# VectorE's small chain behind the products with v, sixteen lead maxima between the last q blocks, the feature DFT with one change of w, wo in query buffers

## The chip, the cores and the metric

The kernel runs on one core of one Trainium2 chip. The metric is device microseconds of one execution: 1841.45 us, the median of 3 runs (1840.29 to 1842.69). A further execution was profiled; it took 1840.34 us, and its span, from the first to the last instruction, is 1838.6 us. Times in the text are microseconds from the start of that span unless a unit is named.

Engines: PE is TensorE (its weight loads are shown apart, as PEld), DVE is VectorE, ACT is ScalarE, POOL is GpSimd, SP is SyncE, which issues every DMA of this kernel from one queue.

## The reference

Everything is float32. x is [2048, 640]. A gate per token mixes a Fourier layer and an attention with 32 heads of 20 columns, which all share one key and one value:

```python
a = jnp.einsum("bsd,ed->bse", x, dft_hid_re)
b = jnp.einsum("bsd,ed->bse", x, dft_hid_im)
y = jnp.einsum("ts,bse->bte", dft_seq_re, a) - jnp.einsum("ts,bse->bte", dft_seq_im, b)

q = (x @ wq) as 32 heads of 20; k = x @ wk; v = x @ wv       # wk, wv: [640, 20]
p = softmax(q k^T * 20 ** -0.5)
o = (p v, heads side by side) @ wo

g = sigmoid((x * gate_w).sum(-1, keepdims=True))
out = g * y + (1 - g) * o
```

wq, wk, wv and wo are drawn 64 times as large as the other weights, so the scores are large and the softmax needs its row maximum.

## The kernel before, in words

**Precision.** float32 values are split into a high and a low part in a faster 32-bit type, and a product is made of three matmuls: high by high, high by low, low by high. A split is a cast and a subtraction, and each operand of a matmul is split once.

**Stages.**

1. The q stage (lines 224 to 352). Four token blocks n of 512. For each: k, v and the gate column (`kv_mm`, `kv_out`), then five q blocks m of 128 columns (`q_mm`, 15 matmuls of 512 columns each), each written to DRAM as a high and a low part (`q_out`). `kv_turn` transposes v. After the last block come `kv_turn(kvT, 3)` and five small instructions for the gate.
2. The lead loop (lines 813 to 828). 240 steps, each with one matmul of the feature DFT on either half of the array (`halves.run`), and spread over them 88 half units of maxima (`a_half`): LEAD is 12, NL is 2 * (32 + 12).
3. 256 rounds (lines 848 to 882): 16 pairs of heads, two query halves, eight steps. The order of TensorE's work within a round is written out by hand as a list (`AB15`, `Y16`, `Y12`, `N12`): bXSn is a half unit of scores, aXSn one of maxima, each on row half X of the array and in PSUM bank Sn, yX one matmul of the DFT, E evicts a finished DFT result, and V is the products with v of an earlier round. The first 48 rounds hold 15 steps of the feature DFT each, the next 144 hold 16 of the sequence DFT, the last 64 hold 12; `N12` is used once no maxima are left.
4. The output projection (lines 889 to 904): 32 groups of 15 matmuls of 320 columns, each evicted by VectorE with the gate and the row of y, and stored.

**Maxima before scores.** A query half v (1024 queries of one pair of heads) has 32 units u, each a block of 128 queries by 512 keys, for two heads. `a_unit` multiplies and VectorE reduces the maximum from PSUM into `mx`. When all 64 halves of v are there, a small chain on VectorE follows: `a_reduce` (L380), then in `a_final` a transpose (L388), a cast (L389) and a subtraction (L390). The result goes to DRAM (`m_d`) and comes back with four DMAs as rows 60, 61, 124 and 125 of `qs[v]`. There it meets keys of -1, so that the score matmul (62 rows) subtracts the maximum, and ScalarE's exponential follows (L735). Maxima run ahead of scores by the lead. In the kernel before, `a_half` puts `a_reduce` one tick and `a_final` two ticks after the last unit; a tick passes with every second half unit of scores.

**The DFT.** The feature DFT runs through four phases, (half, e): which 1024 tokens, and which 320 of the output columns. A change of e needs the other columns of the matrix w, loaded and split by GpSimd (`load_w`, `split_w`, L188 and L189). The order was (1,0), (1,1), (0,1), (0,0). The first phase is the lead loop, the other three the first 48 rounds. Results of half 1 are stored to DRAM and read back for the second half of the sequence DFT.

**Order.** TensorE, ScalarE, VectorE and GpSimd run in the order of the program. SyncE's order is laid out by the framework's scheduler, which may issue a transfer ahead of others that stand before it in the program; waits between instructions are also the framework's, by the memory that they touch.

**wo.** In the last half of the last pair, `BEFORE` lists what follows which of the eight rounds: `load_wo` for three blocks and then two, each with its DMA and its split on VectorE, the loads of the attention output (`load_o`), its multiplication by the reciprocal sums on GpSimd (`mult_o`) and its split (`split_o`, L507 and L508). The raw blocks of wo lay in `spare` tiles, two of them in the slots of the sequence DFT's matrix blocks.

Of the kernel before, what the change touches and what calls it, by code (L numbers as in the profile page):

```python
# [33 lines left out]
def kernel(  # L34
# [165 lines left out]

    PHASES = ((1, 0), (1, 1), (0, 1), (0, 0))
    XSEQ = [SJ * half + j for half, e in PHASES for j in range(SJ)]
# [21 lines left out]
    with ExitStack() as c1:  # L224
# [59 lines left out]

        def kv_turn(kvT, n):
# [8 lines left out]
            nc.vector.tensor_copy(  # L294
                gz[:, ns].rearrange("p (j o) -> p j o", o=1), pv[:, :, 2 * DH : 2 * DH + 1]
            )


        load_x1(0, 0)
# [22 lines left out]
        for n in range(1, 4):  # L322
            for c in range(KC):
                load_x1(n + 1, c)
            pkv = rot(f"kv_{n}")
            for c in range(KC):
                kv_mm(pkv, n, c)
            kv_turn(kvT, n - 1)
            kvT = kv_out(pkv, n)
# [16 lines left out]
        kv_turn(kvT, 3)  # L346

        nc.vector.tensor_scalar_max(gz, gz, -87.0)
        nc.scalar.activation(omg, gz, AF.Exp, scale=-1.0)
        nc.vector.tensor_scalar_add(omg, omg, 1.0)  # L350
        nc.vector.reciprocal(gate, omg)
        nc.vector.tensor_scalar(omg, gate, -1.0, 1.0, op0=ALU.mult, op1=ALU.add)


    abp = ctx.enter_context(tc.tile_pool(name="abp", bufs=1))
    sml = ctx.enter_context(tc.tile_pool(name="sml", bufs=2))

    mx = {}
    QB = NT // 2
    UV = 4 * QB  # L360

    def a_unit(u, hh, tag="A"):

        v, r = divmod(u, UV)
        qb, c = divmod(r, 4)
        if r == 0 and v not in mx:
            mx[v] = sml.tile([P, 2, QB, 4], F32, name="mx")
        b = 64 * hh
        ps = bank(tag, f"a_{u}_{hh}")
        nc.tensor.matmul(  # L370
            ps,
            qs[v][b : b + 60, qb * P : (qb + 1) * P],
            ks[b : b + 60, c * ROW : (c + 1) * ROW],
            start=True,
            stop=True,
        )
        nc.vector.tensor_reduce(mx[v][:, hh, qb, c : c + 1], ps, axis=AX.X, op=ALU.max)  # L377

    def a_reduce(v):
        nc.vector.tensor_reduce(  # L380
            mxr[v % 2][:, : 2 * QB], mx.pop(v).rearrange("p h q c -> p (h q) c"), axis=AX.X, op=ALU.max
        )

    def a_final(v):

        mt = sml.tile([P, 32], F32, name="mt")
        ms = sml.tile([P, 2, 32], F32R, name="ms")
        nc.vector.transpose(mt, mxr[v % 2])  # L388
        nc.vector.tensor_copy(ms[:, 0], mt)  # L389
        nc.vector.tensor_tensor(ms[:, 1], mt, ms[:, 0].bitcast(F32), op=ALU.subtract)  # L390
        move(m_d[v], ms)

        m_v = m_d[v].rearrange("(g r) i t -> r i g t", g=4)
        for hh in range(2):
            for i in range(2):
                r = 64 * hh + 60 + i
                move(
                    qs[v][r : r + 1].rearrange("o (b g t) -> o b g t", g=4, t=32),
                    m_v[hh * QB : (hh + 1) * QB, i : i + 1].rearrange("b o g t -> o b g t"),
                )  # L400


    clock = {"n": 0}
    todo = []

    def later(n, f, *args):
        todo.append((clock["n"] + n, f, args))

    def tick():
        clock["n"] += 1  # L410
        due = [t for t in todo if t[0] <= clock["n"]]
        todo[:] = [t for t in todo if t[0] > clock["n"]]
        for _, f, args in due:
            f(*args)

    NA = NPAIR * 64
    state = [0, 0]

    def a_half(hh, tag="A"):
        u = state[hh]  # L420
        if u >= NA:
            return
        a_unit(u, hh, tag)
        state[hh] = u + 1
        if state[1 - hh] <= u:
            return
        v, r = divmod(u, UV)
        if r == 8 and v + 1 < 2 * NPAIR:
            load_qs(v + 1)
        if r == UV - 1:  # L430
            later(1, a_reduce, v)
            later(2, a_final, v)


# [25 lines left out]
    def spare(k, name):  # L460
        if k % 4 < 2:
            return yp[0].tile([P, D], F32, tag=f"spare{k % 4}", name=name, bufs=1)
        return c_slot(k % 4, [P, D], F32, name)

    def load_wo(cs):
        for c in cs:
            raw = spare(c, "woraw")
            move(raw, wo[c * P : (c + 1) * P])
            t = abp.tile([P, 2, D], F32R, tag=f"ab{c}0", name=f"wo{c}")
            split_w = (t[:, 0], t[:, 1])  # L470
            nc.vector.tensor_copy(split_w[0], raw)
            nc.vector.tensor_tensor(split_w[1], raw, split_w[0].bitcast(F32), op=ALU.subtract)
            wos[c] = split_w

# [43 lines left out]
    def o_group(tb, e):  # L518
# [5 lines left out]
        for c in range(KC):  # L524
            mm3(ps, h[:, c, tk], l[:, c, tk], wos[c][0][:, es], wos[c][1][:, es], KC, c)
        oy = yp[0].tile([P, HALF], F32, tag=("yt", "yu")[e], name="oy")
# [221 lines left out]
    def finish_half(p, qh):  # L748
# [86 lines left out]
    def plan_of(n):  # L835
# [5 lines left out]

    BEFORE = {
        4: (lambda: load_wo(range(3)), lambda: load_o(0), lambda: load_o(1)),
        5: (lambda: load_wo(range(3, KC)), lambda: mult_o(0), lambda: mult_o(1)),
        6: (lambda: split_o(0), lambda: load_o(2)),
        7: (lambda: [load_y(tb) for tb in range(4)],),
    }
    old = []

    for rnd in ROUNDS:  # L850
# [29 lines left out]
        if p == LAST and qh == 1:  # L880
            for f in BEFORE.get(kk, ()):
                f()
    for g in range(2):
# [68 lines left out]
```

## Time and profile before

| what | value |
|---|---|
| median of 3 runs | 1841.45 us |
| profiled execution | 1840.34 us |
| its span | 1838.6 us |
| TensorE busy in it | 1804.0 us |
| VectorE, ScalarE, GpSimd busy | 1391.0, 1235.0, 555.3 us |
| products with v of round 1 start at | 173.28 us |
| products with v of the last round | 1752.74 us |

A line of a timeline or of a group reads: start and duration in us, engine, line of the kernel, operation, what it writes <- what it reads, shapes as partitions x elements, count; in brackets the idle time of the engine just before it and what ended that. A line of windows reads: from and to, length, the busy time of PE, PEld, DVE, ACT and POOL with their instructions, the granted TensorE clock (1 is full), DMA share and GB/s. "SPq" is SyncE's queue; in its lines of waits stand the total, the number and the longest.

### The profile page before, as it was taken

What the parts mean: (1) busy time and instruction counts of PE and PEld (TensorE: products, weight loads), DVE (VectorE), ACT (ScalarE), POOL (GpSimd) and SP (SyncE); (2) the same over time, 40 slices, a digit from 0 to 9 for tenths busy, and PEclk for the clock granted to TensorE, in tenths of its full rate; (3) what the DMA queues carried; (4) which work ended last, traced back from release to release, by engine and by line L of the source; (5) the groups of instructions that cost most, each with busy time, mean ns of one, the idle gap of its engine ahead of it and who ended that gap; (6) DMA issues with size and microseconds to landing.
All of it is one profiled execution on the core that took longest, in us unless ns stands there. A gap on an engine that the chain in (4) does not pass through costs nothing.

```text
span 1838.6 us, 42883 instructions
## 1 busy us (share of the span) xinstructions
PE 1804.0 (98%) x17112; PEld 1298.8 (71%) x17112; DVE 1391.0 (76%) x2313; ACT 1235.0 (67%) x2422; POOL 555.3 (30%) x495
## 2 busy tenths in 40 slices
PE   8998999999999999999999999999999999999989
PEld 6787667767767776777667767776776666666679
DVE  4387888888887888788878888888888888888144
ACT  3335777777777777677767767777777777777810
POOL 3057555665312122122221222222221222111122
PEclk9998999999999999999999999999999999999999
DMA  7643321121221112111111452212221112111366
GB/s 248 195 159 124 118 83 49 41 75 57 78 69 46 58 58 63 54 55 46 61 57 48 141 195 73 74 61 60 60 65 52 52 44 63 52 50 32 108 202 209
DMA packets 107300, 158.08 MB, mean 86 GB/s; under 512 B 25172, under 2 KB 76116, under 8 KB 106500
## 3 DMA queue, kind: packets, MB, share of 16 engines
q1 hardware_dynamic: 107100, 155.34, 26.8%
q8 instruction: 134, 2.20, 0.5%
q14 instruction: 66, 0.54, 0.1%
HBM read 110.80 MB, written 48.76 MB: 87 GB/s over the span
## 4 chain that ended last, share of the span: by engine, by line
PE 84%; DVE 7%; issue 5%; DMA 2%; POOL 1%; SPq 1%; ACT 0%; POOLq 0%; ACTq 0%; DVEq 0%
PE av L739 24%; PE y L545 19%; PE b L727 17%; PE a L370 13%; PE ab L545 5%; DVE mx L377 5%; PE o L116 1%; PE o L114 1%; PE o L115 1%; SPq L106 1%; PE q L114 1%; PE q L116 1%; PE q L115 1%; DVE ms L390 0%; DVE ms L389 0%
## 5 line engine op out<-in xcount | busy, mean ns | idle before, releaser
L377 DVE TENSOR_REDUCE mx<-a 128x1 f32<-128x512 f32 x2048 | 1277.8, 683 | 295.0 <-PE a L370 258.5
L735 ACT ACTIVATE pt<-b 128x512 f32<-128x512 f32 x2048 | 1076.4, 603 | 383.0 <-PE a L370 296.2
L727 PE MATMUL b<-qs,ks 62*128 62x512 f32 x2048 | 775.0, 417 | 10.9 <-DVE mx L377 8.1
L370 PE MATMUL a<-ks,qs 60*128 60x512 f32 x2048 | 732.5, 414 | 6.3 <-DVE mx L377 3.9
L545 PE MATMUL y<-ab,ch 64*128 64x320 f32 x4096 | 722.2, 307 | 0.0
L545 PEld LDWEIGHTS y<-ab,ch 64*128 64x128 f32 x4096 | 549.6, 185 | 10.0
L727 PEld LDWEIGHTS b<-qs,ks 62*128 62x128 f32 x2048 | 350.9, 185 | 242.4 <-DVE mx L377 198.9
L545 PE MATMUL y<-ab,cl 64*128 64x320 f32 x2048 | 510.2, 306 | 0.0
L739 PE MATMUL av<-pt,vsb 128*32 128x512 f32 x4096 | 492.9, 599 | 0.0
L370 PEld LDWEIGHTS a<-ks,qs 60*128 60x128 f32 x2048 | 353.0, 185 | 16.1 <-DVE mx L377 4.6
L545 PEld LDWEIGHTS y<-ab,cl 64*128 64x128 f32 x2048 | 320.9, 185 | 6.4
L555 POOL TENSOR_TENSOR yt<-yt,yu 128x320 f32<-128x320 f32 x64 | 55.8, 872 | 720.8 <-ACT yu L550 710.2
L739 PEld LDWEIGHTS av<-pt,vsb 128*32 128x32 f32 x4096 | 106.9, 109 | 224.1 <-issue 215.6
L447 POOL TENSOR_TENSOR cl<-craw,ch 128x1024 fp32r<-128x1024 f32 x62 | 148.1, 2389 | 5.0
L446 POOL CAST ch<-craw 128x1024 fp32r<-128x1024 f32 x62 | 64.5, 1041 | 262.7 <-PE y L545 209.6
L567 POOL TENSOR_TENSOR abt<-abt,abu 128x320 f32<-128x320 f32 x64 | 55.7, 871 | 143.3 <-ACT abu L589 143.3
L545 PE MATMUL ab<-wbh,xh 64*128 64x320 f32 x256 | 61.6, 310 | 0.0
L545 PE MATMUL ab<-wbh,xl 64*128 64x320 f32 x256 | 61.1, 309 | 0.0
L572 POOL TENSOR_TENSOR ab<-abt,ab 128x320 fp32r<-128x320 f32 x64 | 56.2, 877 | 13.1 <-ACT ab L571 6.4
L114 PE MATMUL o<-wo,osp 128*128 128x320 f32 x160 | 50.5, 315 | 4.5 <-DVE osp L507 4.5
L545 PE MATMUL ab<-w0l,xh 64*128 64x320 f32 x192 | 53.6, 317 | 1.0 <-POOL w0l L189 1.0
L545 PE MATMUL ab<-w1l,xh 64*128 64x320 f32 x192 | 51.8, 308 | 0.0
(96 smaller groups left out, 1466.6 us busy)
## 6 DMA issues: line engine op xcount, KB each, us to landing
craw<-in_cre_dram SPq DMA_DIRECT2D x32, 512.0 KB
craw<-in_cim_dram SPq DMA_DIRECT2D x32, 512.0 KB
xraw<-in_xT_dram SPq DMA_DIRECT2D x32, 320.0 KB
qs<-qh_d SPq DMA_DIRECT2D x128, 80.0 KB
ab_d<-ab SPq DMA_DIRECT2D x16, 640.0 KB
y_d<-yt SPq DMA_DIRECT2D x64, 160.0 KB
ab<-ab_d SPq DMA_DIRECT2D x16, 640.0 KB
xr<-in_xT_dram SPq DMA_DIRECT2D x20, 256.0 KB
```

The lines of the kernel that those rows point to most:

```text
L114: nc.tensor.matmul(ps, wh, xh, start=(i == 0), stop=False)
L370: nc.tensor.matmul(ps, qs[v][b : b + 60, qb * P : (qb + 1) * P], ks[b : b + 60, c * ROW : (c + 1) * ROW], start=True, stop=True,)
L377: nc.vector.tensor_reduce(mx[v][:, hh, qb, c : c + 1], ps, axis=AX.X, op=ALU.max)
L446: eng.tensor_copy(h, raw)
L447: eng.tensor_tensor(l, raw, h.bitcast(F32), op=ALU.subtract)
L545: nc.tensor.matmul(ps, w, x, start=start, stop=stop)
L555: nc.gpsimd.tensor_tensor(yt, yt, yu, op=ALU.add)
L567: nc.gpsimd.tensor_tensor(t0, t0, t1, op=ALU.add)
L572: nc.gpsimd.tensor_tensor(lo, t0, hi.bitcast(F32), op=ALU.subtract)
L727: nc.tensor.matmul(ps, ks[b : b + 62, kc * P : (kc + 1) * P], qs[2 * p + qc // 2][b : b + 62, (qc % 2) * ROW : (qc % 2 + 1) * ROW], start= ...
L735: nc.scalar.activation(t, ps, AF.Exp, scale=SCALE)
L739: nc.tensor.matmul(ps[32 * g : 32 * g + 32, :], vsb[:, kc, :], t, start=first, stop=last)
```

## The change

- `mx` comes from an early pool (`qsp`, two tiles) instead of `sml`, and the functions of the maxima move up in the program. During the last token block, after each of the first four q blocks, four half units of maxima are issued (16 in all), in banks S1 to S4; q blocks and transposes of this block keep to F1, V, S0 and F0. `kv_turn(kvT, 3)` and the gate's instructions follow the second q block.
- LEAD is 10: 84 half units run ahead, 68 of them in the lead loop.
- The order of phases is (1,0), (0,0), (1,1), (0,1).
- `a_reduce`, `a_final` and `finish_sums` go into a list `chores`, which is worked off after each `av_step` (V) of a round; in the lead loop it is worked off at once.
- wo's raw blocks take turns in two tiles; loads and splits stand apart, from round 0 to round 5 of the last half. The split parts of blocks 0 to 2 lie in the first three query buffers and a free slot of the sequence DFT's blocks, those of 3 and 4 in two `ab` tiles.

```diff
-    PHASES = ((1, 0), (1, 1), (0, 1), (0, 0))
+    PHASES = ((1, 0), (0, 0), (1, 1), (0, 1))
...
-            mx[v] = sml.tile([P, 2, QB, 4], F32, name="mx")
+            mx[v] = qsp.tile([P, 2, QB, 4], F32, tag=f"mx{v % 2}", name="mx", bufs=1)
...
+    chores = []
+
+    def do_chores():
+        while chores:
+            f, *args = chores.pop(0)
+            f(*args)
...
         if r == UV - 1:
-            later(1, a_reduce, v)
-            later(2, a_final, v)
+            chores.append((a_reduce, v))
+            chores.append((a_final, v))
+            if not stage["loop"]:
+                do_chores()
...
+            if n == 3:
+                rot = Rot(["F1", "V", "S0", "F0", "F1", "V", "S0", "F0"])
             pkv = rot(f"kv_{n}")
...
                 q_out(ps, n, m)
+                if n == 3 and m < KC - 1:
+                    for z in range(4):
+                        a_half(z % 2, f"S{1 + z}")
+                    if m == 1:
+                        kv_turn(kvT, 3, rot)
+                        gate_out()
...
+        return cpool.tile([P, D], F32, tag=f"raw{k % 4 - 2}", name=name)
+
+    wo_raw = {}
+
+    def load_wo(c):
+        wo_raw[c] = spare(c % 2, "woraw")
+        move(wo_raw[c], wo[c * P : (c + 1) * P])
+
+    def split_wo(c):
+        raw = wo_raw.pop(c)
+        if c < 3:
+            if c == 0:
+                wos["at"] = [t[:, : 3 * HALF] for t in qbuf[:3]]
+                wos["at"].append(c_slot(2 * free_c[0], [P, 3 * HALF], F32R, "wo"))
+            at = [wos["at"][k // 3][:, k % 3 * HALF : (k % 3 + 1) * HALF] for k in range(4 * c, 4 * c + 4)]
+        else:
+            t = abp.tile([P, 4, HALF], F32R, tag=f"ab{c - 3}0", name=f"wo{c}")
+            at = [t[:, k] for k in range(4)]
+        for e in range(2):
+            h, l, r = at[2 * e], at[2 * e + 1], raw[:, e * HALF : (e + 1) * HALF]
+            nc.vector.tensor_copy(h, r)
+            nc.vector.tensor_tensor(l, r, h.bitcast(F32), op=ALU.subtract)
+            wos[c, e] = (h, l)
...
-            later(24, finish_sums, p, sm)
+            later(24, chores.append, (finish_sums, p, sm))
...
-    LEAD = 12
+    LEAD = 10
...
-    done = 0
+    done = first = 2 * state[0]
...
-        while done < NL * n // KL:
+        while done < first + (NL - first) * n // KL:
...
     BEFORE = {
-        4: (lambda: load_wo(range(3)), lambda: load_o(0), lambda: load_o(1)),
-        5: (lambda: load_wo(range(3, KC)), lambda: mult_o(0), lambda: mult_o(1)),
-        6: (lambda: split_o(0), lambda: load_o(2)),
-        7: (lambda: [load_y(tb) for tb in range(4)],),
+        0: ((load_wo, 0), (load_wo, 1)),
+        1: ((split_wo, 0), (split_wo, 1), (load_wo, 2)),
+        2: ((load_wo, 3), (split_wo, 2)),
+        3: ((load_wo, 4),),
+        4: ((split_wo, 3), (load_o, 0), (load_o, 1)),
+        5: ((split_wo, 4), (mult_o, 0), (mult_o, 1)),
+        6: ((split_o, 0), (load_o, 2)),
+        7: tuple((load_y, tb) for tb in range(4)),
     }
...
                     av_step(*st)
+                    do_chores()
```

More of the change, by code (lines that the diff above doesn't have):

```diff
@@ L199, in w_of, with later, tick, a_unit @@
         return h[:, c], l[:, c]
-    PHASES = ((1, 0), (1, 1), (0, 1), (0, 0))
+    clock = {"n": 0}
+    todo = []
+    def later(n, f, *args):
+        todo.append((clock["n"] + n, f, args))
+    def tick():
+        clock["n"] += 1
+        due = [t for t in todo if t[0] <= clock["n"]]
+        todo[:] = [t for t in todo if t[0] > clock["n"]]
+        for _, f, args in due:
+            f(*args)
+    mx = {}
+    QB = NT // 2
+    UV = 4 * QB
+    def a_unit(u, hh, tag="A"):
+        v, r = divmod(u, UV)
+        qb, c = divmod(r, 4)
+        if r == 0 and v not in mx:
+            mx[v] = qsp.tile([P, 2, QB, 4], F32, tag=f"mx{v % 2}", name="mx", bufs=1)
+        b = 64 * hh
+        ps = bank(tag, f"a_{u}_{hh}")
+        nc.tensor.matmul(
+            ps,
+            qs[v][b : b + 60, qb * P : (qb + 1) * P],
+            ks[b : b + 60, c * ROW : (c + 1) * ROW],
+            start=True,
+            stop=True,
+        )
+        nc.vector.tensor_reduce(mx[v][:, hh, qb, c : c + 1], ps, axis=AX.X, op=ALU.max)
@@ new lines, in a_reduce, with a_final @@
+    def a_reduce(v):
+        nc.vector.tensor_reduce(
+            mxr[v % 2][:, : 2 * QB], mx.pop(v).rearrange("p h q c -> p (h q) c"), axis=AX.X, op=ALU.max
+        )
+    def a_final(v):
+        mt = sml[0].tile([P, 32], F32, name="mt")
+        ms = sml[0].tile([P, 2, 32], F32R, name="ms")
+        nc.vector.transpose(mt, mxr[v % 2])
+        nc.vector.tensor_copy(ms[:, 0], mt)
+        nc.vector.tensor_tensor(ms[:, 1], mt, ms[:, 0].bitcast(F32), op=ALU.subtract)
+        move(m_d[v], ms)
+        m_v = m_d[v].rearrange("(g r) i t -> r i g t", g=4)
+        for hh in range(2):
+            for i in range(2):
+                r = 64 * hh + 60 + i
+                move(
+                    qs[v][r : r + 1].rearrange("o (b g t) -> o b g t", g=4, t=32),
+                    m_v[hh * QB : (hh + 1) * QB, i : i + 1].rearrange("b o g t -> o b g t"),
+                )
@@ L296, in kv_turn, with gate_out @@
             )
+        def gate_out():
+            nc.vector.tensor_scalar_max(gz, gz, -87.0)
+            nc.scalar.activation(omg, gz, AF.Exp, scale=-1.0)
+            nc.vector.tensor_scalar_add(omg, omg, 1.0)
+            nc.vector.reciprocal(gate, omg)
+            nc.vector.tensor_scalar(omg, gate, -1.0, 1.0, op0=ALU.mult, op1=ALU.add)
         load_x1(0, 0)
@@ L379, in a_reduce @@
[L379 to L400, printed above, removed]
@@ L435 @@
+    sml.append(ctx.enter_context(tc.tile_pool(name="sml", bufs=2)))
     free_c = [0, 1, 2]
@@ L880 @@
         if p == LAST and qh == 1:
-            for f in BEFORE.get(kk, ()):
-                f()
+            for f, n in BEFORE[kk]:
+                f(n)
     for g in range(2):
```

80 lines of the change are left out of this document (19 added, 61 removed).

## The prediction

> **What bounds the kernel now.** I read the page first, then windows by stage, then the timelines of the windows that stood out.
>
> ```profile
> span 1838.6 us, 42883 instructions
> PE 1804.0 (98%) x17112; PEld 1298.8 (71%) x17112; DVE 1391.0 (76%) x2313; ACT 1235.0 (67%) x2422; POOL 555.3 (30%) x495
> PE 84%; DVE 7%; issue 5%; DMA 2%; POOL 1%; SPq 1%; ACT 0%; POOLq 0%; ACTq 0%; DVEq 0%
> ```
>
> TensorE sets the end, yet its 98% busy says little: two half-array matmuls overlap, so a late start hides as long as anything runs. Losses show in start times. The profiled execution took 1840.34 us, its span 1838.6 plus 1.7 around it; the median of the runs shown is 1841.45, 1.1 above. The sum below starts from 1840.34.
>
> The pace of one matmul with 320 columns comes from the output projection, where each result closes 15 of them; the pace of one round comes from the last rounds, which hold no maxima:
>
> ```profile
> 1826.34 0.55 DVE L527 SCALAR_TENSOR_TENSOR oy<-o,omg,yrow 128x320 f32<-128x320 f32 x1 [1.65 <-PE o L116]
> 1828.54 0.55 DVE L527 SCALAR_TENSOR_TENSOR oy<-o,omg,yrow 128x320 f32<-128x320 f32 x1 [1.65 <-PE o L116]
> ...
> 1747.99 1.92 PE L739 MATMUL av<-pt,vsb 128*32 128x512 f32 x16
> 1749.85 0.73 PE L727 MATMUL b<-qs,ks 62*128 62x512 f32 x4
> 1752.74 1.92 PE L739 MATMUL av<-pt,vsb 128*32 128x512 f32 x16
> ```
>
> 2.20/15 = 0.147 us a matmul. Sixteen products with v hold TensorE 1.86 us (1747.99 to 1749.85), four score halves at most 0.73, and such a round takes 4.75.
>
> **Part 1: sixteen lead maxima go between the q blocks.** The lead stage:
>
> ```profile
> 97.43 0.69 DVE L263 TENSOR_TENSOR ql<-q,qh 128x512 fp32r<-128x512 f32 x1 [2.81 <-ACT qh L262]
> 101.80 3.08 DVE L377 TENSOR_REDUCE mx<-a 128x1 f32<-128x512 f32 x5 [2.44 <-DMA qs<-qh_d]
> 102.55 0.49 PE L370 MATMUL a<-ks,qs 60*128 60x512 f32 x1 [3.27 <-DVE mx L377]
> 106.62 0.19 PEld L370 LDWEIGHTS a<-ks,qs 60*128 60x128 f32 x1
> 110.42 0.18 PEld L370 LDWEIGHTS a<-ks,qs 60*128 60x128 f32 x1
> 106.00:155.00 49.00, 48.35 (x521) 46.37 (x518) 48.89 (x84) 22.23 (x51) 35.92 (x37) 1.00 0.45 150
> ```
>
> The stage opens with a hole: the first maximum waits for a transfer until 101.80 and TensorE for it until 102.55. The maxima are written to a tile of a pool opened after the q stage's pools closed; I read the wait as one for memory that the last transfers still read. The change moves this tile to an early pool. From 106 to 155 the third busy figure, VectorE's, is 48.89 of 49: the lead is VectorE's, at (3.08-0.68)/4 = 0.60 us a maximum, times 88 = 53.
>
> Afterwards the lead holds 84-16 = 68 maxima: 41 us of VectorE, and TensorE decides. Its own price of a maximum comes from 106.62 to 110.42, before VectorE was behind: 7 maxima in 3.80 us, each with 240/88 = 2.73 steps of 0.147, leaves 0.142 a maximum. So 240 x 0.147 + 68 x 0.142 = 44.9; with the small chain once inside I take 45.5. Before, the lead ran from about 0.65 ahead of the last ql (97.43) to the first score at 155.32, below: 58.5. **-13.0** (-7.2 if each maximum had the array alone for 0.147 x 512/320 = 0.235 us, its columns at the pace above: 35.3 + 16.0 = 51.3; -13.6 without the chain). I take the measured 0.142, since it is the same pair of matmuls in the same loop.
>
> The 16 moved maxima cost TensorE 4 x (4 x 0.142 to 0.73) = 2.3 to 2.9: **+2.3**. VectorE has 2.81 us idle ahead of each ql, and four reductions take 2.4, so they hide; without that cover each q block would be 2.4 later. The small gate chain moved there adds about 1 once, and VectorE catches up in the last block.
>
> **Part 2: one change of w instead of two.** The first change fell on the start of the rounds:
>
> ```profile
> 155.32 0.49 PE L727 MATMUL b<-qs,ks 62*128 62x512 f32 x1 [0.28 <-ACT abt L589]
> 158.04 0.63 PE L545 MATMUL ab<-w0l,xh 64*128 64x320 f32 x1 [0.97 <-POOL w0l L189]
> 173.28 1.07 PE L739 MATMUL av<-pt,vsb 128*32 128x512 f32 x8
> ```
>
> GpSimd splits the new w only after the lead, TensorE waits for it, then for what had queued up. From the first score to the products with v of round 1 pass 17.96 us. An undisturbed round of this stage takes 6.15 (286.22 to 292.37 below), 4.29 without its products with v; round 0 has none, so two such bodies are 8.6. Now w keeps its half over the first two phases: **-9.4**. The remaining change comes at round 16, inside the loop. Before, one stood at round 32 with nothing longer around it, so I cost it at zero; its cover is a whole round between split and use, and without that it costs the same 9.4. Four loads and their eight GpSimd instructions go; none of the others was on the deciding path, and the SyncE queue is only the shorter for it.
>
> **Part 3: VectorE's small chain behind the products with v.** Every eighth round has it. Products with v, by stage, then VectorE and GpSimd:
>
> ```profile
> 286.22 1.92 PE L739 MATMUL av<-pt,vsb 128*32 128x512 f32 x16
> 292.37 1.92 PE L739 MATMUL av<-pt,vsb 128*32 128x512 f32 x16
> 299.47 1.07 PE L739 MATMUL av<-pt,vsb 128*32 128x512 f32 x8
> ...
> 696.03 1.92 PE L739 MATMUL av<-pt,vsb 128*32 128x512 f32 x16
> 702.76 1.50 PE L739 MATMUL av<-pt,vsb 128*32 128x512 f32 x12
> 709.03 1.92 PE L739 MATMUL av<-pt,vsb 128*32 128x512 f32 x16
> ...
> 1502.31 1.92 PE L739 MATMUL av<-pt,vsb 128*32 128x512 f32 x16
> 1508.90 1.92 PE L739 MATMUL av<-pt,vsb 128*32 128x512 f32 x16
> 1514.95 1.50 PE L739 MATMUL av<-pt,vsb 128*32 128x512 f32 x12
> ```
>
> ```profile
> 697.45 0.22 DVE L380 TENSOR_REDUCE mxr<-mx 128x16 f32<-128x64 f32 x1
> ...
> 699.67 0.20 DVE L388 STREAM_TRANSPOSE mt<-mxr 128x32 f32<-128x32 f32 x1
> ...
> 700.12 0.19 DVE L390 TENSOR_TENSOR ms<-mt,ms 128x32 fp32r<-128x32 f32 x1
> ...
> 705.18 1.29 DVE L377 TENSOR_REDUCE mx<-a 128x1 f32<-128x512 f32 x2 [1.04 <-PE a L370]
> ```
>
> The same chain's cast once, inside the lead, and GpSimd beside it:
>
> ```profile
> 142.00 0.87 POOL L567 TENSOR_TENSOR abt<-abt,abu 128x320 f32<-128x320 f32 x1
> ...
> 142.47 0.45 DVE L389 CAST ms<-mt 128x32 fp32r<-128x32 f32 x1
> ```
>
> A round with the chain is longer by 7.10-6.15 = 0.95 (6 rounds with the feature DFT), 6.73-6.27 = 0.46 (18 rounds of 16 steps), 6.59-6.05 = 0.54 (6 of 12): 5.7+8.3+3.2 = 17.2 us. The chain takes 0.22 + 0.64 = 0.86; the idle time under the products with v is 1.04. Placed there it fits if nothing lengthens it. What can is GpSimd: the cast at 142.47 took 0.45 and ended with GpSimd's sum (142.87). In the DFT rounds GpSimd sums right behind the evictions, at the same time as the moved chain, in each round; of the 18 a third (a result closes every 48/16 = 3 rounds). I take half of 5.7, 6.5 of 8.3 and all of 3.2: **-12.5**, between 0 and -17.2.
>
> [...]
>
> Queued behind the chain are the rows of maxima, which SyncE writes out and reads back before the scores:
>
> ```profile
> 700.34 0.32 SPq L106 DMA_DIRECT2D m_d<-ms  x1
> 701.79 2.73 SPq L106 DMA_DIRECT2D qs<-m_d  x4
> 717.17 0.50 PE L727 MATMUL b<-qs,ks 62*128 62x512 f32 x1
> SPq L106 <- POOL yt L559: 249.9, 30, 17.1
> ```
>
> The chain ended at 700.31; now it starts at 704.14 and ends at 705.0. The last read was issued by 704.52; taking for its landing the 1.45 between the write's issue and the first read, the path is 5.7 us, so the rows stand at 710.7, 6.5 ahead of 717.17. No cost. The reciprocals of the sums (one per pair of heads) move to the same place, later by less than a round, and fall in other rounds; the three transfers behind each are read only by the output projection.
>
> **Part 4: wo in query buffers.** The end of the rounds:
>
> ```profile
> 1753.23 0.49 DVE L471 CAST wo<-woraw 128x640 fp32r<-128x640 f32 x1 [22.98 <-DMA woraw<-in_wo_dram]
> 1759.19 0.60 PE L114 MATMUL o<-wo,osp 128*128 128x320 f32 x1 [4.53 <-DVE osp L507]
> 1766.62 0.41 PE L114 MATMUL o<-wo,osp 128*128 128x320 f32 x1
> 1754.60:1766.60 12.00, 6.91 (x35) 4.37 (x31) 8.64 (x9) 0.63 (x2) 3.87 (x3) 0.72 0.60 180
> ```
>
> VectorE sits before wo's third block until 1753.23 (its raw buffer was one of the last c blocks'), splits three blocks, then the first output columns; TensorE waits 4.53 and then runs at a granted clock of 0.72. With wo split by round 5 of the last eight, the first group can start at 1752.74 + 1.86 = 1754.60, take 15 x 0.147 = 2.2, the last products 1.86, and the second group starts at 1758.66 instead of 1766.62: **-8.0**. All transfers behind it, and so the later waits, move up with it. The five loads now pass SyncE ahead of the last sums and their reciprocals, and each of the later three waits there for a split; if one holds the queue, part of the wait returns (0 to -8). I take the whole, since VectorE was idle 22.98 us ahead of 1753.23, which covers all five splits.
>
> **Part 5: LEAD 10.** Four halves fewer lead, so one round of 4.75 becomes a part-filled one of at most 6.05: **+0.6** (0 to 1.3).
>
> **Sum:** 2.3 - 13.0 - 9.4 - 12.5 + 0.6 - 8.0 = -40.0; 1840.3 - 40.0 = 1800.3, on the median's footing 1801.
>
> **Rivals.**
> *Port held* (8 in 100): GpSimd's operations hold the cast and the subtraction in every round but the last six, and only 3.2 of part 3 comes: 9.3 more, 1811. For: 142.47. Against: two thirds of the 18 have no result to sum there.
> *Lead slower* (8): each maximum alone on the array, or GpSimd behind: 51.3 instead of 45.5, 1807. For: GpSimd was busy 35.92 of 49 already. Against: the 0.142.
> *Maxima before their keys* (8): the last keys are computed just ahead of these q blocks; if the maxima wait for all of them, TensorE stands about as long as ahead of 102.55, 3.27, and loses half as much again while its clock is low: 1806. For: the maxima stand ahead of the next q block in TensorE's order, so a wait stops that too. Against: of the first eight halves only two need them, and these stand behind the second q block.
> *The change of w keeps its price* at round 16 (6): 1811. For: 158.04. Against: no such wait at round 32.
> *Tail's next wait* (7): SyncE or the multiplication by the reciprocals is late, half of part 4 lost: 1805. For: 22.98 shows one late load holding all. Against: the new raw buffers are free from the start of the last half.
> *Rows late, slower* (4): SyncE takes its transfers in order, and holds for GpSimd's results 249.9/30 = 8.3 us at a time. If the write or read of each of the 31 later groups of maxima falls behind such a hold, it exceeds the 6.5 spare by 1.8: 56 us, 1857. It outweighs the gain from a mean hold of 6.5 + 40/31 = 7.8. Against: the old order met the 1.45 of 700.34 without one.
>
> **Numbers.** The forecast itself has 59 in 100, with 1793 to 1808 of its own (the whole 17.2 of the chain gives 1797, with the other ends of parts 1 and 5 1795; half of the lead's doubt and no DFT-stage chain gain give 1807). The range 1791 to 1815 takes in the middle rivals and two of them together. A measurement of this kernel tells 0.2%, some 3.7 us, from no change. Faster 0.94; same 0.02 (several rivals at once); slower 0.04.
>
> **What would show it.** No hole before the first lead maximum and a lead of some 45 us; no GpSimd wait at the first rounds; chain rounds at most 0.3 longer than their neighbours outside the DFT stage; output matmuls right behind the last round at full clock. Wrong if scores wait for rows of maxima, if a stall stands at round 16, or if VectorE still fills the lead.

## The result and the profile after

The changed kernel takes **1818.18 us**, the median of 4 runs (1817.05 to 1819.99), beside 1840.87 for the kernel before in the same comparison: a ratio of **0.9876, 95% interval 0.9859 to 0.9894**. It is 22.7 us faster where the forecast had 40, and it lies 3.2 us above the range. The profiled execution took 1818.21 us. Its page, with the chain that ended last:

```profile
span 1816.4 us, 42871 instructions
PE 1794.3 (99%) x17112; PEld 1288.5 (71%) x17112; DVE 1412.8 (78%) x2323; ACT 1233.9 (68%) x2422; POOL 545.3 (30%) x487
PE 92%; DVE 5%; POOL 1%; DMA 1%; issue 0%; ACT 0%; SPq 0%; POOLq 0%
```

TensorE's busy time says little again. As before, the account goes by start times. The table cuts both spans at the same marks: the first matmul of the feature DFT, the first score, and the products with v of chosen rounds.

| from, to | start before | start after | length before | length after | difference | forecast |
|---|---|---|---|---|---|---|
| start to the lead | 0 | 0 | 96.78 | 100.59 | +3.8 | +2.3 |
| lead, to the first score | 96.78 | 100.59 | 58.54 | 48.70 | -9.8 | -13.0 |
| to the first products with v | 155.32 | 149.30 | 17.95 | 11.18 | -6.8 | -9.4 |
| 46 rounds with the feature DFT | 173.28 | 160.48 | 288.65 | 286.60 | -2.1 | -2.9 |
| 144 rounds of 16 steps | 461.93 | 447.08 | 912.08 | 907.16 | -4.9 | -6.5 |
| 50 rounds of 12 steps | 1374.01 | 1354.24 | 306.55 | 309.26 | +2.7 | -3.2 |
| the last 14 rounds | 1680.56 | 1663.50 | 72.18 | 75.07 | +2.9 | +0.6 |
| to the end | 1752.74 | 1738.57 | 85.82 | 77.87 | -8.0 | -8.0 |

The lengths add up to the two spans, and the differences to -22.1. One line has the wrong sign, the 50 rounds of 12 steps; together with the 14 rounds behind them it lies 8.2 behind the forecast. Of the +3.8 at the start 0.9, and of the +2.9 of the last 14 rounds 1.6, are no part of the change: there, from 19.06 and from 1671.11, the granted clock was at half for 3.41 us (the last section says more on it). The timeline of the changed kernel around its lead, VectorE and TensorE:

```profile
101.38 0.69 DVE L350 TENSOR_TENSOR ql<-q,qh 128x512 fp32r<-128x512 f32 x1 [1.28 <-ACT qh L349]
101.99 6.11 DVE L233 TENSOR_REDUCE mx<-a 128x1 f32<-128x512 f32 x10
...
136.92 0.49 PE L226 MATMUL a<-ks,qs 60*128 60x512 f32 x1 [0.92 <-DVE mx L233]
...
149.30 0.50 PE L757 MATMUL b<-qs,ks 62*128 62x512 f32 x1 [1.64 <-ACT abt L619]
...
151.75 0.50 PE L226 MATMUL a<-ks,qs 60*128 60x512 f32 x1 [0.91 <-ACT pt L765]
```

The hole ahead of the lead's first maximum is gone: it follows the last ql at once. VectorE no longer quite fills the lead; the windows view gives it 40.98 of 43:

```profile
106.00:149.00 43.00, 40.74 (x484) 38.68 (x480) 40.98 (x66) 20.39 (x51) 34.61 (x36) 1.00 0.47 158
```

TensorE's starts stand still twice in the lead: 1.2 us ahead of 136.92, behind the small chain, and 2.0 ahead of 149.30, where the first score waits for an eviction. Without these 3.2 the lead would be 45.5. The forecast had 44.9 without the chain and allowed 0.6 for it; the second stall was missing from it. Products with v in the changed kernel, around one round with the small chain in each stage (the chain follows the second of each three lines, so its round lies between the second and the third):

```profile
228.68 1.93 PE L769 MATMUL av<-pt,vsb 128*32 128x512 f32 x16
234.82 1.92 PE L769 MATMUL av<-pt,vsb 128*32 128x512 f32 x16
241.51 1.92 PE L769 MATMUL av<-pt,vsb 128*32 128x512 f32 x16
...
478.45 1.92 PE L769 MATMUL av<-pt,vsb 128*32 128x512 f32 x16
484.74 1.92 PE L769 MATMUL av<-pt,vsb 128*32 128x512 f32 x16
491.64 0.64 PE L769 MATMUL av<-pt,vsb 128*32 128x512 f32 x4
...
1483.59 1.92 PE L769 MATMUL av<-pt,vsb 128*32 128x512 f32 x16
1489.67 1.92 PE L769 MATMUL av<-pt,vsb 128*32 128x512 f32 x16
1496.72 1.92 PE L769 MATMUL av<-pt,vsb 128*32 128x512 f32 x16
```

A chain round takes 6.69 where its neighbours take 6.14 (six times in the DFT stage), 6.90 against 6.29 (four times of 18, the other fourteen cost nothing), and 7.05 against 6.08, six times: in the last stage it costs about 1.0, where the old order cost 0.55. The timeline of that last chain, GpSimd's instructions beside VectorE's:

```profile
1489.44 1.04 POOL L464 CAST ch<-craw 128x1024 fp32r<-128x1024 f32 x1 [8.44 <-PE y L575]
1490.56 2.38 POOL L465 TENSOR_TENSOR cl<-craw,ch 128x1024 fp32r<-128x1024 f32 x1
1490.81 0.21 DVE L236 TENSOR_REDUCE mxr<-mx 128x16 f32<-128x64 f32 x1
...
1491.30 1.68 DVE L245 CAST ms<-mt 128x32 fp32r<-128x32 f32 x1
...
1493.01 0.19 DVE L246 TENSOR_TENSOR ms<-mt,ms 128x32 fp32r<-128x32 f32 x1
...
1493.86 0.49 PE L757 MATMUL b<-qs,ks 62*128 62x512 f32 x1 [0.60 <-DVE mx L233]
```

The cast of 128x32 takes 1.68 instead of 0.18 and ends at 1492.98. GpSimd's subtraction of the c split ends at 1492.94. The maxima queued behind the cast are late, and TensorE's next score waits for one of them. In the four dear rounds of 16 steps a sum of GpSimd holds the cast (0.46 at 789.21) and GpSimd's cast of c holds the subtraction (0.96 at 789.71, up to 790.67; GpSimd's cast ends at 790.62). In the DFT rounds it is GpSimd's sum that does the same, and then its cast holds VectorE's subtraction:

```profile
236.50 0.87 POOL L597 TENSOR_TENSOR abt<-abt,abu 128x320 f32<-128x320 f32 x1 [1.50 <-ACT abu L619]
...
236.61 0.81 DVE L245 CAST ms<-mt 128x32 fp32r<-128x32 f32 x1
...
237.44 0.49 DVE L246 TENSOR_TENSOR ms<-mt,ms 128x32 fp32r<-128x32 f32 x1
237.44 0.45 POOL L599 CAST ab<-abt 128x320 fp32r<-128x320 f32 x1
```

The end of the rounds:

```profile
1738.57 1.92 PE L769 MATMUL av<-pt,vsb 128*32 128x512 f32 x16
1740.42 0.42 PE L114 MATMUL o<-qs,osp 128*128 128x320 f32 x1
...
1742.82 1.92 PE L769 MATMUL av<-pt,vsb 128*32 128x512 f32 x16
1744.67 0.41 PE L114 MATMUL o<-qs,osp 128*128 128x320 f32 x1
```

The output products follow the last round without a pause, and the second group starts 6.10 behind the last products with v of the rounds (5.92 in the forecast).

### The profile page after: what moved, and what is told of

Same layout as the page of the kernel before. It is cut to its first block, busy times and chain, and to the rows that moved or that the text cites. A ratio compares the mean times of both kernels' runs of the same rounds, so it can differ in the third digit from the quotient of the medians.

```text
span 1816.4 us, 42871 instructions
## 1 busy us (share of the span) xinstructions
PE 1794.3 (99%) x17112; PEld 1288.5 (71%) x17112; DVE 1412.8 (78%) x2323; ACT 1233.9 (68%) x2422; POOL 545.3 (30%) x487
## 4 chain that ended last, share of the span: by engine, by line
PE 92%; DVE 5%; POOL 1%; DMA 1%; issue 0%; ACT 0%; SPq 0%; POOLq 0%
PE av L769 25%; PE y L575 21%; PE b L757 18%; PE a L226 14%; PE ab L575 6%; DVE mx L233 3%; PE o L114 1%; PE o L116 1%; PE o L115 1%; PE q L114 1%; PE q L116 1%; PE q L115 1%; DVE ms L245 1%; POOL ab L602 1%; POOL abt L597 1%; DVE ms L246 0%
## 5 line engine op out<-in xcount | busy, mean ns | idle before, releaser
L226 PE MATMUL a<-ks,qs 60*128 60x512 f32 x2048 | 722.9, 411 | 2.4 <-DVE mx L233 0.9
L575 PE MATMUL ab<-w0h,xh 64*128 64x320 f32 x192 | 49.2, 311 | 0.0
```

The costliest lines, as they stand in the source:

```text
L226: nc.tensor.matmul(ps, qs[v][b : b + 60, qb * P : (qb + 1) * P], ks[b : b + 60, c * ROW : (c + 1) * ROW], start=True, stop=True,)
L575: nc.tensor.matmul(ps, w, x, start=start, stop=stop)
```

## The experiments

Medians are of 4 or 5 runs each; the kernel before had medians of 1841.9, 1840.9 and 1842.8 in the three comparisons, so a difference of 2 between medians of two comparisons says little by itself. Differences of a stage are read in the profiled runs, between the same marks as in the table.

**The chain's place and LEAD.** Four kernels have the two places of the chain with the two values of LEAD. The first puts the chain back:

```diff
-            chores.append((a_reduce, v))
-            chores.append((a_final, v))
+            later(1, a_reduce, v)
+            later(2, a_final, v)
...
-            later(24, chores.append, (finish_sums, p, sm))
+            later(24, finish_sums, p, sm)
```

> The changed kernel, but VectorE's small chain goes back to its old places among the maxima (and the reciprocals with it). Theory A (the port: GpSimd's instructions lengthen the moved chain's cast and subtraction, so that the new place kept most of the old price): in the DFT stage +2.1, in the rounds of 16 steps +4.9, in those of 12 steps -2.7, in all +4, 1822. Theory B (the forecast: the move alone is worth 12.5, and the missing time lies elsewhere): 1831. A result at 1818 would say that the move did nothing at all.

1814.19 (1813.87 to 1816.79): 4 below the changed kernel, a result that neither theory had. The rounds of 16 and of 12 steps are as long as in the changed kernel (906.91 and 309.33), the DFT rounds 3.0 shorter; another 1.6 is the clock, which did not fall in the last rounds here (1.00 in the windows from 1665 to 1673). So at LEAD 10 the moved order saves nothing over the old one, and the 4.9 that the 16-step rounds gained against the kernel before is not the new order's alone. What else had changed for these rounds was LEAD.

```diff
-    LEAD = 10
+    LEAD = 12
```

> The changed kernel with LEAD 12 instead of 10: two units more lead, and every chain falls one round earlier. Theory A (port, and a lead that is GpSimd's): the chains of the 12-step rounds leave GpSimd's split of c: -5 to -6; the part-filled round at the end goes, -1.4; the four more maxima in the lead cost nothing as GpSimd sets its pace: in all -6 to -8, 1811. Rival 1 (the 1.0 of a chain round with 12 steps does not hang on the split of c): -1.4, 1817. Rival 2 (the lead is TensorE's or VectorE's): 4 x 0.142 to 4 x 0.60 more in the lead on either theory, +0.6 to +2.4.

**1806.91** (1806.31 to 1808.51): 11.3 below the changed kernel, more than theory A had. The 12-step rounds lose 6.1, the 16-step rounds 2.9: no chain round there is longer than its neighbours by more than chance. The timeline of a chain in the 12-step rounds, with GpSimd's split behind it:

```profile
1480.77 0.18 DVE L245 CAST ms<-mt 128x32 fp32r<-128x32 f32 x1
1480.99 0.19 DVE L246 TENSOR_TENSOR ms<-mt,ms 128x32 fp32r<-128x32 f32 x1
...
1484.76 1.04 POOL L464 CAST ch<-craw 128x1024 fp32r<-128x1024 f32 x1 [8.37 <-PE y L575]
...
1485.88 2.38 POOL L465 TENSOR_TENSOR cl<-craw,ch 128x1024 fp32r<-128x1024 f32 x1
...
1487.45 3.70 DVE L233 TENSOR_REDUCE mx<-a 128x1 f32<-128x512 f32 x6 [1.17 <-PE b L757]
```

A round takes four units of maxima and a group needs 32. With 12 units ahead a group ends with a round; with 10 it ends two units into the next one, and its chain falls one round later. In the 12-step rounds that is just the round, one in four, in which GpSimd splits c. Here the chain stands one round ahead of it.

> The changed kernel with the small chain in its old places and LEAD 12: with the three runs before it, all four pairs of chain place and LEAD. Theory C (LEAD sets where the chain falls in a round and beside what of GpSimd, so the two parts cannot be added up: at LEAD 12 the old places cost what they cost before, and the move saves nearly all of it): the chain rounds show 0.95, 0.46 and 0.55 again, 17.2 less the 3.1 that the run with LEAD 12 still has: 14 above it, 1821. Rival (the other parts of the change took the chain's price away, and LEAD 10 alone brings prices of its own, whatever the order): 1807 to 1810, with chain rounds no longer than their neighbours.

The edit is the two above together. **1820.51** (1819.44 to 1821.26), as theory C had it: the chain rounds show 7.10, 6.73 and 6.59 again, the lengths of the kernel before. The two of them as medians, and the sum of the 240 rounds of the first three stages in brackets:

| | LEAD 10 | LEAD 12 |
|---|---|---|
| chain in its old places | 1814.19 (1499.8) | 1820.51 (1507.9) |
| chain at the products with v | 1818.18 (1503.0) | 1806.91 (1493.9) |

So the move is worth 14.1 of the rounds at LEAD 12 and costs 3.2 at LEAD 10. The groups of the chain's cast say why. Least, median and greatest duration in ns of 32 casts, first with the old places and LEAD 12, then moved with LEAD 12, then the changed kernel:

```profile
L245 DVE CAST ms<-mt x32: 181/182/293, 132.6 to 1689.4; 128x32 fp32r<-128x32 f32 x32
```

```profile
L245 DVE CAST ms<-mt x32: 180/220/676, 131.6 to 1678.4; 128x32 fp32r<-128x32 f32 x32
```

```profile
L245 DVE CAST ms<-mt x32: 180/457/1774, 134.6 to 1691.6; 128x32 fp32r<-128x32 f32 x32
```

In the old places at LEAD 12 the casts are hardly held; there the chain's plain time stands ahead of maxima that TensorE needs. At the products with v it has cover, and what it costs is what GpSimd adds. LEAD 10 chooses the rounds in which GpSimd adds most.

**The chain off VectorE's held instructions.**

```diff
-        nc.vector.tensor_copy(ms[:, 0], mt)
-        nc.vector.tensor_tensor(ms[:, 1], mt, ms[:, 0].bitcast(F32), op=ALU.subtract)
+        nc.gpsimd.tensor_copy(ms[:, 0], mt)
+        nc.gpsimd.tensor_tensor(ms[:, 1], mt, ms[:, 0].bitcast(F32), op=ALU.subtract)
```

> The changed kernel, but the chain's cast and subtraction run on GpSimd, so that only the reduction and the transpose (0.4 together, nothing held) stay on VectorE. Theory A (the port): what is left of the chain's price goes, 6 x 0.53 in the DFT stage, 4 x 0.62 with 16 steps, 6 x 1.0 with 12 steps: -11.7, 1806.5, if the rows of maxima still come in time; they now queue on GpSimd behind its splits of c (3.4 us) where the spare time is 4 to 8 us. Rival 1 (the place itself costs, VectorE's time there and not the port): only two unheld operations of 0.19 in those 16 rounds, -2 to -4, 1815. Rival 2 (rows late): b waits for rows in the rounds after the split of c, 6 x some 2 us, 1818 or more.

**1806.25** (1805.85 to 1807.09), 0.25 from theory A. The three stages of rounds are 3.1, 2.7 and 6.1 shorter, and chain rounds are as long as their neighbours: 6.05 for the round that took 7.05.

```profile
1483.63 1.92 PE L769 MATMUL av<-pt,vsb 128*32 128x512 f32 x16
1489.67 1.93 PE L769 MATMUL av<-pt,vsb 128*32 128x512 f32 x16
1495.72 0.64 PE L769 MATMUL av<-pt,vsb 128*32 128x512 f32 x4
```

This edit takes two unheld operations of 0.2 from VectorE as well. That those cost nothing at the products with v, the run with LEAD 12 has shown.

> LEAD 12 and the chain's cast and subtraction on GpSimd together. Theory (the port is all that is left of the chain's price): the six chain rounds of the DFT stage lose their last 0.5, no chain round is longer than its neighbours in any stage, and the end has no part-filled round: 2.9 below the run with LEAD 12, 1.3 below the one with the chain on GpSimd: 1804 to 1805. Rival (the two savings are the same time, counted twice elsewhere): 1806 to 1807.

1804.55 (1802.74 to 1805.40), within the theory's 1804 to 1805: 2.4 below LEAD 12 alone. Its DFT rounds take 283.43 in place of 286.41. The chain has no price left.

**The lead's end.** Two kernels change the order of the operations behind each DFT group of the lead. The first delays only GpSimd's low part; the new ab_low issues the subtraction of the group before:

```diff
         nc.gpsimd.tensor_tensor(t0, t0, t1, op=ALU.add)
+        ab_low()
...
             nc.scalar.activation(hi, t0, AF.Copy)
-        nc.gpsimd.tensor_tensor(lo, t0, hi.bitcast(F32), op=ALU.subtract)
+        lows.append((lo, t0, hi, (t - SJ, e) if half == 1 and i == 1 else None))
```

> The changed kernel, but in the lead GpSimd's low part of a group is issued behind the sum of the next group, so that GpSimd need not wait for ScalarE's cast in between (0.58 us idle in each of 16 groups). Theory A (the lead is GpSimd's): the lead falls from 48.7 to the 45 to 46 that TensorE needs, and with less left over on GpSimd the first round is up to 2 us shorter: 1813 to 1815. Rival (TensorE, each maximum alone on the array, or VectorE sets the lead): no change, 1818.

1817.87 (1816.18 to 1822.03), the rival's number. The lead did not shorten: 50.07 in the profiled run, with a longer wait at its end. GpSimd's idle time in front of the low part was therefore not what set the lead. The wait goes round between two engines: ScalarE's evictions, which free TensorE's banks, stand behind its cast of the sum, and the cast waits for GpSimd's sum of the evictions before (ahead of the last two casts of the changed kernel's lead ScalarE waits 2.08 and 1.15 for it). The second kernel delays the cast as well; its ab_low issues the cast and the subtraction of the group before:

```diff
         nc.gpsimd.tensor_tensor(t0, t0, t1, op=ALU.add)
+        ab_low()
+        if not stage["loop"]:
+            late.append((hi, lo, t0, (t - SJ, e) if half == 1 and i == 1 else None))
+            return
```

> The changed kernel, but in the lead ScalarE's cast and GpSimd's low part of a group are both issued behind the next group's evictions and sum. Theory (at the lead's end TensorE waits 2.03 and 1.22 for banks whose eviction stands on ScalarE behind a cast, which waits for GpSimd's sum): both waits go, the lead ends some 2 to 3 earlier, and the first round starts without a pause: 1815 to 1816. Rival (GpSimd has too much left over at the lead's end whatever the order): the wait only moves to the first rounds, 1818.

**1812.70** (1812.53 to 1812.94): 5.5 less, more than expected, and for other reasons. The lead takes 46.62, 2.1 less, and the stalls of 1.2 in it and behind the first score are gone. The first score's wait, which should have gone, is still there, longer, and so is that of the eviction ahead of it:

```profile
146.13 0.44 ACT L631 ACTIVATE abt<-ab 128x320 f32<-128x320 f32 x1 [1.49 <-POOL ab L600]
...
146.62 0.50 PE L769 MATMUL b<-qs,ks 62*128 62x512 f32 x1 [2.20 <-ACT abt L631]
```

The eviction now waits for a buffer that GpSimd's low part (L600) holds, so at the lead's end GpSimd is behind in either order, as the rival had it. Of the rest, 1.6 lies at the last rounds, where the clock did not fall (the mean granted clock of 0.999 leaves some 3.6 us at half, and 3.4 of them stand in the windows from 146 to 152), and 1.4 is spread over the rounds of the first two stages; its cause stays open.

**The sixteen maxima.**

```diff
-                    for z in range(4):
-                        a_half(z % 2, f"S{1 + z}")
```

> The changed kernel without the 16 maxima between the q blocks; all 84 are in the lead again, their tile stays in the early pool. Theory D (the lead's gain came from the early pool, which closed the hole ahead of the first maximum, and the 16 maxima cost between the q blocks, 3.8, about what they save): the lead takes 240 x 0.147 + 84 x 0.142 = 47.2 for TensorE, but 84 x 0.60 = 50.4 for VectorE, 2 to 4 more than now, and starts 3.8 earlier: 1816 to 1819. The forecast (they cost 2.3 and save the difference of 53 and 45.5): 5 more, 1823.

1816.28 (1815.90 to 1817.76), as theory D had it. The lead starts 2.9 earlier (97.69) and takes 3.1 more (51.83); the rest of the gain is put down to the clock in the last rounds again (the mean granted clock is 0.999, and 0.998 in the changed kernel). The lead is VectorE's in this kernel, by the windows view 42.71 of 43:

```profile
106.00:149.00 43.00, 42.26 (x471) 41.25 (x469) 42.71 (x75) 19.89 (x46) 32.98 (x34) 1.00 0.47 161
```

Against the 58.54 of before, the lead is 6.7 shorter even without the sixteen. Four maxima fewer are 2.4 of that at VectorE's 0.60 each. The other 4.3 is about the hole: before, VectorE stood from the end of the last ql, 98.12, to 101.80; here the first maximum follows the last ql at once (99.08). That the early pool closed the hole is inferred; no run moves that tile alone. The sixteen maxima between the q blocks cost what they save.

**The order of phases.**

```diff
-    PHASES = ((1, 0), (0, 0), (1, 1), (0, 1))
+    PHASES = ((1, 0), (1, 1), (0, 1), (0, 0))
```

> The changed kernel with the old order of phases, so w changes twice again, the first time at the lead's end. Theory (the changed order is what made the way from the first score to round 1's products with v 6.8 shorter): that way takes 17 to 18 us again, 1825; the change of w at round 16 goes, which costs nothing either way. Rival (that way is shorter because less is left over on GpSimd and ScalarE after the new lead, for instance four halves fewer): within 2 of 1818.

1823.42 (1823.20 to 1824.62), 5.2 more; the way from the first score to the first products with v takes 18.62 instead of 11.18, and TensorE's waits there are those for w again:

```profile
149.77 0.41 PE L575 MATMUL ab<-w0h,xh 64*128 64x320 f32 x1 [0.82 <-POOL w0h L188]
152.06 0.63 PE L575 MATMUL ab<-w0l,xh 64*128 64x320 f32 x1 [1.74 <-POOL w0l L189]
156.14 0.79 PE L226 MATMUL a<-ks,qs 60*128 60x512 f32 x1 [2.38 <-ACT pt L765]
```

The part is worth 7.4 where it stands. Some of that is the clock: it was at half for 10.24 us of this way with the old order (the run's mean granted clock is 0.997) and not at all in the changed kernel (1.00 in the windows from 146 to 164). In the other kernels with the new order the way took 10.8 to 13.6, and 16.24 with the low part alone delayed, where the clock was at half for longest (13.6 us by its windows from 152 to 168). The run as a whole shows 5.2, and its span 5.0, because the clock fell neither at the start (lead 0.7 earlier) nor in the last 14 rounds (73.48 and not 75.07).

**wo.** The old loading and splitting, with the last three of five splits behind the last rounds:

```diff
-        0: ((load_wo, 0), (load_wo, 1)),
-        1: ((split_wo, 0), (split_wo, 1), (load_wo, 2)),
...
+        4: (lambda: load_wo(range(3)), lambda: load_o(0), lambda: load_o(1)),
+        5: (lambda: load_wo(range(3, KC)), lambda: mult_o(0), lambda: mult_o(1)),
```

> The changed kernel with the old loading and splitting of wo. Theory (the tail's 8.0 is all of this part): from the last products with v to the end 85.9 again, 1826. Rival (half of the tail's gain is due to other transfers that moved): 1822.

1826.42 (1824.26 to 1827.90): 8.2 more, the theory's 1826. In the profiled run, which took 1827.44, the way to the end is 87.17 instead of 77.87, and TensorE waits 5.39 for the first output columns.

**Put together.** LEAD 12, the chain's cast and subtraction on GpSimd, no maxima between the q blocks, and the later casts and low parts in the lead:

> LEAD 12, the chain's cast and subtraction on GpSimd, no maxima between the q blocks, and the later casts and low parts in the lead, together. If these add up: 1806.9 - 2.9 - 1.9 - 2 = 1800, with 1798 to 1804 by whether the clock stays up at the lead's end. If the lead, with all 84 maxima, is VectorE's, the last two give nothing: 1804.

1804.28 (1803.33 to 1804.88): the second case. At LEAD 12 it is 88 maxima, not 84, that all stand in the lead; it takes 53.75, and what its earlier start and the other order give is lost there. The next kernel differs in one line, by which VectorE no longer makes the last splits of c:

```diff
-        eng = nc.vector if last else nc.gpsimd
+        eng = nc.gpsimd
```

> As before it, and the last splits of c on GpSimd like all others, not on VectorE. Theory (the round of 7.9 near the end is 1.85 longer because VectorE's split stands ahead of its maxima): that round takes 6.05, 1.85 less than the kernel before it. Rival (GpSimd's split takes 3.4 us, and the products with c wait for it): as much lost there as won.

**1802.45** (1801.34 to 1803.72), a ratio to the kernel before of 0.9784 (0.9771 to 0.9798); it is faster than both kernels. The round took 7.89 and now takes 6.06:

```profile
1651.50 1.92 PE L779 MATMUL av<-pt,vsb 128*32 128x512 f32 x16
1657.56 1.92 PE L779 MATMUL av<-pt,vsb 128*32 128x512 f32 x16
1663.61 0.64 PE L779 MATMUL av<-pt,vsb 128*32 128x512 f32 x4
```

LEAD 12, the chain on GpSimd, the order of the casts and the sixteen maxima kept, all in one kernel, was not tried.

## Why the prediction was wrong

The step that failed is **part 5**. It priced LEAD 10 by a count: four halves fewer, one part-filled round, +0.6. With the chain at the products with v it measured +11.3 by the medians. In the profiled spans it is 9.7, of which 9.2 lie in the 240 rounds of the first three stages, since LEAD also decides in which round a chain falls, and so beside which of GpSimd's instructions. The part-filled round took 6.01 in place of 4.75, the 1.3 that the forecast had as its worst case. Parts 3 and 5 were summed as if independent, and they are not: with the chain in its old places the same LEAD 10 saved 6.3. The run with LEAD 12, 1806.9, lies inside the range given. Of the 17.9 that are missing between the two spans, parts 3 and 5 have 10.6, part 1 has 4.7 and part 2 has 2.6.

**Part 3** was right in its mechanism and near in its size, at the LEAD for which its rows stood: -14.1 where -12.5 was forecast. By stage, LEAD 12, against the same kernel in the old order: -2.0 in the DFT rounds (forecast -2.9), -8.8 in the 16-step rounds (-6.5), -3.3 in the 12-step rounds (-3.2). The near total hides that the 16-step rounds gave more and the DFT rounds less than forecast. The forecast looked for GpSimd's sums there. The instruction that mattered most was its split of c, 3.5 us long and in every fourth of the 12-step rounds, which the text never set beside the chain: with a chain every eighth round, LEAD decides whether all six meet it or none. In the changed kernel parts 3 and 5 together gave -4.3 in the rounds and +1.3 at the end; the other 1.6 there is the clock.

**Part 1** was too large by the stalls. TensorE's own 44.9 is right to 0.6, but two stalls of 1.2 and 2.0 come on top, where the forecast allowed 0.6: one behind the chain held in the lead, one for the eviction at the end. The rival *Lead slower* named GpSimd for it, with 51.3; it was 48.7, and the stall stands at the end, where ScalarE and GpSimd hand the banks back, not in the pace. The +2.3 was 2.9 by the run without the sixteen maxima, the upper end given; the other 0.9 of the 3.8 is put down to the clock, at half for 3.41 us from 19.06 on. With LEAD 12 the lead starts at 99.64. The hole was read rightly, and the run without the sixteen maxima shows that they gave none of the gain: by the working above, the closed hole and four maxima fewer account for it.

**Part 2** was right in kind. It is worth some 7, not 9.4: what had queued up on ScalarE and GpSimd at the lead's end is there without the change of w too, and TensorE still waits 0.91 in the first round (151.75). No stall stands at round 16 (its rounds take 6.15), so *the change of w keeps its price* is out.

**Part 4** held: 85.82 to 77.87, 8.0; *tail's next wait* did not come.

*Port held* (GpSimd's operations hold the cast and the subtraction), given 8 in 100 and 1811, is the rival that came, in a place and with a holder that it did not have: it left out the last six chain rounds, and those cost most, by the split of c. The row it cited (the cast of 0.45 beside GpSimd's sum) was the sign. *Rows late* did not come. In the list of TensorE's waits of the changed kernel no transfer of maxima and none of the DFT's w appears; beside two waits of the lead's end and the first round (1.6 and 0.9) and the one behind the lead's chain (0.9), what remains behind the q stage is this, total, times and the longest:

```profile
PE b L757 <- DVE mx L233: 7.1, 12, 1.5
```

One small sum of the ranges is off as well: the whole 17.2 of the chain makes the forecast's 1801 into 1796, not 1797. Nothing hangs on it.

## What to carry to other kernels

A constant that says how far one stage runs ahead also sets the phase of everything periodic behind it: before its cost is counted, lay the beat of the moved work beside the beat of each engine's long instructions. Two parts of a change that touch the same beat are priced together, or tried at both values. A cast of 0.18 on VectorE that began beside GpSimd's subtraction of 2.38 took 1.68 here and ended 0.04 behind it; keep the two in different rounds (with LEAD 12 the kernel took 11.3 less), or give the short one to GpSimd (11.9 less).

## What the runs showed of the hardware

**VectorE's casts waited for GpSimd here, its maxima did not.** The cast of 0.18 took 1.68 and ended 0.04 behind GpSimd's subtraction. Of the chain's 64 casts and subtractions in the changed kernel 30 took over 0.25, and each of these ended 0.03 to 0.05 behind an instruction of GpSimd. Six maxima that begin beside such a subtraction (1487.45, LEAD 12, the subtraction to 1488.26) took 3.70, 0.62 each; ten in the lead took 6.11. Of the changed kernel's maxima 142 lie wholly inside a subtraction of c: none took over 0.69, nor did any other. These read PSUM, but the chain's own reduction, which reads `mx` and not PSUM, took 0.21 inside such a subtraction too (1490.81). The two operations of the chain on GpSimd itself take 0.21 and 0.25 in the median, hardly more than VectorE's 0.18 and 0.19 where it did not wait:

```profile
L245 POOL CAST ms<-mt x32: 205/211/618, 138.1 to 1680.1; 128x32 fp32r<-128x32 f32 x32
```

**The clock halved behind a short pause in one execution and not in others.** Near the end TensorE waits for VectorE's last split of c. The windows of the changed kernel behind that wait, the granted clock in the third column from the right:

```profile
1668.00:1670.00 2.00, 0.51 (x6) 0.28 (x5) 2.00 (x3) 0.50 (x2) 0.00 (x0) 1.00 0.00 0
1670.00:1672.00 2.00, 2.00 (x18) 1.31 (x20) 2.00 (x5) 1.42 (x3) 0.00 (x0) 0.78 0.64 164
1672.00:1674.00 2.00, 2.00 (x12) 0.39 (x8) 0.66 (x2) 0.26 (x1) 0.00 (x0) 0.50 0.01 4
1674.00:1676.00 2.00, 2.00 (x20) 1.09 (x12) 0.57 (x1) 0.54 (x2) 0.00 (x0) 0.87 0.00 0
```

The round there takes 7.47 in place of 6.05. The same pause stands in the kernel before (1.49, up to 1686.79) and with the old places at either LEAD, and there the clock stays at 1.00. With the low part delayed the waits at the lead's end were longer (from 148 to 152 TensorE is busy for 1.43 us, and for 1.79 in the changed kernel), and the clock stayed at half for some 12 us:

```profile
154.00:166.00 12.00, 10.67 (x68) 9.85 (x66) 7.58 (x12) 7.01 (x13) 6.28 (x7) 0.50 0.33 125
```

In the changed kernel's trace the granted clock falls to half at 19.06 and 1671.11, for 3.41 us each time; in the kernel before it falls at 102.90 (behind the wait of 3.27), 157.51 and 1758.36, for 3.41, 10.24 and 6.83. Within each of the two executions the changes lie whole multiples of 3.413 us apart (from 19.06 to 1671.11 it is 484 of them). The pause near the end begins 0.54 behind such a mark in the changed kernel, where the clock fell, and 2.03 behind one in the kernel before, where it did not. That the place decides is an inference from these two; what else the clock goes by was not shown. The stretch near the end cost the changed kernel 1.4 us.
